# Half-row score products in two banks, and the planner's order for the whole program

## The chip, the cores and the metric

The kernel runs on one core of a Trainium2 chip. The metric is the device time of one execution in microseconds. The kernel before takes 1044.72 us, the median of 3 runs (1044.53 to 1045.08).

## The reference

Attention over a window of 128 positions with a bias by distance, then a feed-forward block (FFN) over the result, all in fp32:

```python
B, H, S, D = 8, 8, 576, 64            # q, k, v: batch, heads, positions, head size
scores = q @ k.T / sqrt(D)            # for each batch and head
scores = where((rel >= 0) & (rel < 128), scores + slope[h] * -abs(rel), -1e9)
attn = softmax(scores)                # over the keys
x = (attn @ v) laid out as [B * S, H * D]       # 4608 x 512
h = x @ w_in                          # 512 x 2048
out = (h * sigmoid(1.702 * h)) @ w_out          # 2048 x 512
```

## The kernel before

**Precision by parts.** TensorE multiplies in fp32r, which is faster than fp32 and rounds its operands. The kernel therefore splits an operand into a rounded high part and the low rest, and adds up several products. In the FFN those are three products per tile (w high with x high, w low with x high, w high with x low; L1074 for the first layer, L1197 for the second, and L1162 in the last chunks, which combine weights first).

**The score products.** A head has 64 dimensions, the array 128 rows. The q and k of a head pair lie in memory twice, once in partitions 0 to 63 and once in 64 to 127. A block is 128 queries with the 256 keys that its window can reach (128 keys for the first block of a sequence). A unit is one or two blocks that are worked on together; a head pair of a batch has 9 blocks, hence 5 units, the last of one block. For each unit the kernel makes the tile Q (rounded q in all partitions, then the low rest of q written over the lower half of the partitions, 64 to 127, L508), K1 (rounded k in both halves) and K2 (the low rest of k in both halves). Each block is then two products on the full array: Q with K1 gives q high times k high plus q low times k high, and Q with K2 adds q high times k low and q low times k low (L853). The two blocks of a unit lie side by side in one bank of PSUM, the tile s_ps, of which there is one.

**After the scores.** VectorE (DVE) adds the bias and finds the row minimum of the negated scores while it reads s_ps (L872), ScalarE (ACT) takes the exponent (L884), the rows are normalised (L907), TensorE transposes them (flip, L928, into one of two t slots of PSUM), ACT and DVE split the transposed tile into high and low (ph, pl, L505 and L947), and TensorE multiplies with V (mix, L973, into x_ps). The sums of head pairs go to the x tiles of the FFN, for later chunks by way of DRAM.

**The first batch** is worked on in plain fp32 (L850 for scores, L967 for the product with V). There the two heads of a pair lie in the two halves of the partitions, so that a score product uses 64 rows of the array, and some of the two heads' products go into two banks, s_ps and s_h.

**The FFN** runs in chunks of 256 tokens over 16 slices of the hidden size: up (12 matmuls into h_ps), the gate (tanh on ACT, L1090; a product on DVE, L1091), the split into gh and gl (L505, L508), down (6 matmuls of 512 columns into two acc banks). The weights come in 8-byte words and are decoded early in the program (w_ps, wc).

**What sets the order.** All work is first added to a list (`Plan.add`) with a duration, the engine, other engines that could do it (`ways`) and what it reads and writes. `Plan.order(CUT)` then plays the list through in its own count of nanoseconds, picks engine, slot and start for each item, and stops at CUT; on PE it takes the item for which `max(free[e], op.ready + SAFE)` is least. What it placed is emitted in that order and stays so. `Plan.rest()` gives out what is left in the order of the list, on the engine named by `auto`, and the framework's scheduler puts these instructions in order by its own simulated timeline. In the kernel before CUT is 340000.

Of the kernel before, what the change touches and what calls it, by code (L numbers as in the profile page):

```python
# [8 lines left out]
F32 = mybir.dt.float32  # L9
# [10 lines left out]
B, H, S, D = 8, 8, 576, 64  # L20
DM, DFF = 512, 2048
NT = B * S
P = 128
HALF = P // 2
NP = H // 2
# [20 lines left out]
GATE = 6  # L46
READY = {"PE": 1600, "DVE": 4400, "ACT": 700, "POOL": 2700, "SP": 700}
HOP = {"PE": 220, "ACT": 60, "DVE": 60, "POOL": 60, "SP": 60}
CUT = 340000
WARM = 7000  # L50
LAX = {"w": 1000, "hi": 800, "lo": 0, "gl": 300, "cast": 0, "xl": 600, "p": 500}
RATE = 330
# [3 lines left out]
MIXED = ("t", "o", "h", "acc1")  # L56
TURN = {}
STICK = 80
SAFE = 60
REST = 400  # L60
FAR = 7
PACE = 32
LATE = 14
FAST = {c: range(0, 7) if c > LATE else range(2, 7) for c in range(LATE, NCH)}
# [202 lines left out]
class Plan:  # L267
# [5 lines left out]
    def add(self, eng, run, ns, lag=100, r=(), w=(), port=False, chain=None, bytes=0, shift=0, ways=None, behind=None, lax=0, auto=None, kind="R", late=None):  # L273
        op = Op(len(self.ops) + shift, eng, run, ns, lag, port)
        op.bytes, op.i = bytes, len(self.ops)
        op.ways.update(ways or {})
        op.lax = lax
        op.auto, op.late = auto or eng, late
        op.kind = kind
        before, after = set(), set()  # L280
        for items, writes in ((r, False), (w, True)):
            for item in items:
                buf, key = item if isinstance(item, tuple) else (item, None)
                if not buf.ops:
                    op.opens.append(buf)
                    if buf.tag not in MIXED:
                        if buf.tag in self.openers:
                            after.add(self.openers[buf.tag])
                        self.openers[buf.tag] = op
                else:  # L290
                    after.add(buf.ops[0])
                buf.ops.append(op)
                buf.left += 1
                op.bufs.append(buf)
                for k in list(buf.last):
                    if meet(key, k):
                        before.add(buf.last[k])
                if writes:
                    for k in list(buf.readers):
                        if meet(key, k):  # L300
                            before.update(buf.readers[k])
                            if key is None or k == key:
                                del buf.readers[k]
                    if key is None:
                        buf.last = {}
                    buf.last[key] = op
                else:
                    buf.readers.setdefault(key, []).append(op)
        if chain is not None:
            if chain in self.chains:  # L310
                after.add(self.chains[chain])
            self.chains[chain] = op
        if behind is not None:
            after.add(behind)
        before.discard(op)
        after -= before | {op}
        for b in sorted(before, key=lambda o: o.i):
            b.next.append((op, True))
        for b in sorted(after, key=lambda o: o.i):
            b.next.append((op, False))  # L320
        op.waits = op.before = len(before) + len(after)
        self.ops.append(op)
        return op
# [141 lines left out]
def tile_kernel(ctx: ExitStack, tc: tile.TileContext, q0, k0, v0, qT, kT, v, w_in, w_out, out):  # L465
    nc = tc.nc
# [9 lines left out]
    add = plan.add  # L476

    def buf(pool, shape, dtype, tag, slots=1, name=None):
        return Buf(plan, pool, shape, dtype, tag, slots, name)
# [9 lines left out]
    def act_cast(n):  # L489
        return 104 + 0.8 * n  # L490
# [10 lines left out]
    def pool_two(n):  # L501
        return 140 + 2.17 * n

    def copy_on(e, dst, src):
        (nc.scalar.copy if e == "ACT" else nc.vector.tensor_copy)(dst, src)  # L505

    def less_on(e, dst, a, b):
        (nc.gpsimd if e == "POOL" else nc.vector).tensor_tensor(dst, a, b, ALU.subtract)  # L508
# [13 lines left out]
    def less_ways(n):  # L522
        return {"DVE": (dve_one(n), True)}
# [246 lines left out]
    def split_q(u):  # L770
        if u.whole:
            return
        u.Q = buf(att, [P, 2 * P], F32R, "Q", 2)
        add("ACT", lambda e: copy_on(e, u.Q.t[:, :u.nq], u.rq.t[:, :u.nq]), act_cast(u.nq), r=[u.rq], w=[u.Q],
            chain="split_q", ways=cast_ways(u.nq), behind=gates[32 * 2 - 1 - 32])

    def split_v(u):
# [10 lines left out]
        for i, c in enumerate(u.loaded):  # L788
            c.vbuf = u.VV
            c.v = lambda i=i, c=c: u.VV.t[:c.n, i].rearrange("p a d -> p (a d)")  # L790

    def split_rest(u):
        if u.whole:
            return
        u.K1 = buf(att, [P, 3 * P], F32R, "K1", 2)
        u.K2 = buf(att, [P, 3 * P], F32R, "K2", 2)
        add("ACT", lambda e: copy_on(e, u.K1.t[:, :u.nk], u.rk.t[:, :u.nk]), act_cast(u.nk),
            r=[u.rk], w=[u.K1], chain="K1", ways=cast_ways(u.nk), auto="DVE")
        add("POOL", lambda e: less_on(
            e, u.Q.t[D:, :u.nq], u.rq.t[D:, :u.nq], u.Q.t[D:, :u.nq].bitcast(F32)), pool_two(u.nq),  # L800
            r=[u.rq], w=[u.Q], port=True, chain="Q", ways=less_ways(u.nq), lax=LAX["lo"])
        add("POOL", lambda e: less_on(
            e, u.K2.t[:, :u.nk], u.rk.t[:, :u.nk], u.K1.t[:, :u.nk].bitcast(F32)), pool_two(u.nk),
            r=[u.rk, u.K1], w=[u.K2], port=True, chain="K2", ways=less_ways(u.nk), lax=LAX["lo"])
# [13 lines left out]

    def scores(u):
        if early(u):  # L820
            u.s = buf(ps, [P, 2, 2 * P], F32, "h", 2, name="s_h")
        else:
            u.s = buf(ps, [P, 2, 2 * P], F32, "s", 1, name="s_ps")
        ns = 0
        runs, reads = [], []
        for e, b in enumerate(u.blocks):
            n = b.end - b.first
            if u.whole:
                lo = b.q0 - u.at
                qr, q = columns(0, u, lo, b.rows)  # L830
                at, k = b.first, lo - P + b.first
                while at < b.end:
                    m = min(b.end - at, T - k % T)
                    kr, ks = columns(1, u, k, m)
                    runs.append((e, b, at, m, q, ks))
                    reads += [r for r in (qr, kr) if r not in reads]
                    ns += max(1.72 * m, 220)
                    at, k = at + m, k + m
            else:
                ko = b.q0 - P + b.first - u.k0  # L840
                qs = slice(b.q0 - u.q0, b.q0 - u.q0 + b.rows)
                ks = slice(ko, ko + n)
                ns += 2 * max(0.465 * n, 86)
                runs.append((e, b, b.first, n, qs, ks))

        def run():
            for e, b, at, n, q, k in runs:
                to = u.s.t[:b.rows, e, at:at + n]
                if u.whole:
                    nc.tensor.matmul(to, q(), k(), start=True, stop=True)  # L850
                else:
                    for z, ks in enumerate((u.K1, u.K2)):
                        nc.tensor.matmul(to, u.Q.t[:, q], ks.t[:, k], start=(z == 0), stop=(z == 1))  # L853

        u.scored = add("PE", run, ns, 165, r=reads if u.whole else [u.Q, u.K1, u.K2], w=[u.s],
            chain="scores", kind="S" if u.whole else "R")
        if early(u):
            u.scored.beside = units[u.n - 1].scored

    def biased(u):  # L860
        u.mins = small(u, 0, "mins")
        for e, b in enumerate(u.blocks):
            if first(u):
                b.p = Part(works[u.n // 2], (u.n % 2, e), lambda t, i=u.n % 2 * 2 + e: t[:, i])
            else:
                b.p = buf(att, [P, 2 * P], F32, "pb", 5)
            for head, ra, rb, cs in b.heads:
                if cs > b.live:
                    add("POOL", lambda b=b, ra=ra, rb=rb, cs=cs: nc.gpsimd.memset(b.p.t[ra:rb, b.live:cs], MOST),
                        230, w=[b.p.key_at()])  # L870
                on = ra if u.joined else 0
                add("DVE", lambda b=b, e=e, head=head, ra=ra, rb=rb, cs=cs, on=on: nc.vector.tensor_tensor_reduce(  # L872
                    b.p.t[ra:rb, cs:b.end], u.s.t[ra:rb, e, cs:b.end], bias[ra:rb, head, on + cs:on + b.end],
                    -SCALE, BIG, ALU.add, ALU.min, u.mins.t[ra:rb, e:e + 1]),
                    75 + 1.05 * (b.end - cs), 150, r=[u.s], w=[b.p.key_at(), u.mins.key_at(e)], chain="biased")
            if b.live > b.first:
                add("POOL", lambda b=b: nc.gpsimd.memset(b.p.t[:, :b.live], 0.0), 120, w=[b.p.key_at("z")])

# [576 lines left out]
```

## Time and profile before

| what | value |
|---|---|
| median of 3 runs | 1044.72 us |
| the profiled execution | 1044.83 us |
| its span, first to last instruction | 1043.0 us |
| busy: PE, DVE, ACT, POOL | 99%, 76%, 63%, 51% |
| granted TensorE clock | 0.999 |
| DMA, mean share of the 16 engines by queue | 31.2% and 2.5%, instructions 0.6% |

A row of a group reads: line, engine, operation, output and inputs, form (rows and columns of the array that a matmul uses, as in 64*128, then the size), count, busy time of the group in microseconds, mean of one in nanoseconds, idle time of the engine ahead of them. The mean of a matmul is its whole way through the array (a matmul of 256 columns shows some 0.28 us); how fast matmuls follow one another is read from their starts. A row of the timeline gives the start, the time to the end of the last one, and the count.

### The profile page before, as it was taken

What the parts mean: (1) busy time and instruction counts of PE and PEld (TensorE: products, weight loads), DVE (VectorE), ACT (ScalarE), POOL (GpSimd) and SP (SyncE); (2) the same over time, 40 slices, a digit from 0 to 9 for tenths busy, and PEclk for the clock granted to TensorE, in tenths of its full rate; (3) what the DMA queues carried; (4) which work ended last, traced back from release to release, by engine and by line L of the source; (5) the groups of instructions that cost most, each with busy time, mean ns of one, the idle gap of its engine ahead of it and who ended that gap; (6) DMA issues with size and microseconds to landing.
All of it is one profiled execution on the core that took longest, in us unless ns stands there. A gap on an engine that the chain in (4) does not pass through costs nothing.

```text
span 1043.0 us, 23177 instructions
## 1 busy us (share of the span) xinstructions
PE 1029.4 (99%) x7220; PEld 937.7 (90%) x7220; DVE 793.5 (76%) x2464; ACT 655.8 (63%) x1962; POOL 530.6 (51%) x804
## 2 busy tenths in 40 slices
PE   9999999999999999999999999999999999999998
PEld 5777888988888999999999999999999999999997
DVE  8999988899978888768686777768766744667574
ACT  7999877677745666666666666666666643344443
POOL 3343445344423467576666757666666623333342
PEclk9999999999999999999999999999999999999999
DMA  9734233333322333434333433424242354001000
GB/s 355 303 96 141 61 88 95 80 81 98 83 76 65 103 101 94 141 90 129 95 114 106 122 104 101 126 76 150 79 117 67 113 169 140 21 22 41 2 22 21
DMA packets 122027, 106.65 MB, mean 102 GB/s; under 512 B 48880, under 2 KB 111984, under 8 KB 121904
## 3 DMA queue, kind: packets, MB, share of 16 engines
q1 hardware_dynamic: 116720, 95.73, 31.2%
q10 hardware_dynamic: 5184, 9.44, 2.5%
q8 instruction: 57, 0.93, 0.4%
q14 instruction: 66, 0.54, 0.2%
HBM read 82.58 MB, written 22.54 MB: 101 GB/s over the span
## 4 chain that ended last, share of the span: by engine, by line
PE 88%; DVE 8%; issue 2%; ACT 2%; POOL 0%; DMA 0%; DVEq 0%; ACTq 0%; POOLq 0%
PE h_ps L1074 35%; PE acc L1197 28%; PE s_ps L853 5%; PE t_ps L928 5%; PE x_ps L973 5%; PE m L1162 3%; PE acc L1162 2%; PE s_ps L850 1%; PE x_ps L967 1%; DVE g L1091 1%; DVE wc L592 1%; DVE pb L872 1%; DVE w_ps L589 1%; PE idle L556 1%; DVE gl L508 1%
## 5 line engine op out<-in xcount | busy, mean ns | idle before, releaser
L1074 PE MATMUL h_ps<-xh,w 128*128 128x256 f32 x2304 | 358.7, 283 | 0.3
L1074 PEld LDWEIGHTS h_ps<-xh,w 128*128 128x128 f32 x2304 | 316.9, 188 | 18.4 <-DVE g L1091 1.7
L1197 PE MATMUL acc<-w,gh 128*128 128x512 f32 x928 | 259.5, 396 | 0.0
L1074 PE MATMUL h_ps<-xl,w 128*128 128x256 f32 x1152 | 187.3, 280 | 0.0
L508 POOL TENSOR_TENSOR gl<-g,gh 128x256 fp32r<-128x256 f32 x169 | 131.7, 781 | 107.5 <-ACT gh L505 68.2
L1197 PEld LDWEIGHTS acc<-w,gh 128*128 128x128 f32 x928 | 157.6, 189 | 19.3 <-issue 0.2
L1074 PEld LDWEIGHTS h_ps<-xl,w 128*128 128x128 f32 x1152 | 158.2, 188 | 2.3
L884 ACT ACTIVATE pb<-pb,mins 128x256 f32<-128x256 f32 (+2 forms) x272 | 132.3, 487 | 39.5 <-DVE mins L872 29.8
L508 POOL TENSOR_TENSOR Q<-rq,Q 64x256 fp32r<-64x256 f32 (+1 forms) x136 | 94.9, 698 | 117.9 <-issue 25.6
L1091 DVE SCALAR_TENSOR_TENSOR g<-g,h_ps 128x256 f32<-128x256 f32 x236 | 97.6, 413 | 72.5 <-ACT g L1090 70.9
L1090 ACT ACTIVATE g<-h_ps 128x256 f32<-128x256 f32 x236 | 90.1, 382 | 92.7 <-PE h_ps L1074 69.7
L1197 PE MATMUL acc<-w,gl 128*128 128x512 f32 x464 | 148.1, 397 | 0.0
L508 POOL TENSOR_TENSOR K<-rk,K 128x384 fp32r<-128x384 f32 (+1 forms) x121 | 109.7, 907 | 69.8 <-ACT Q L505 23.8
L505 ACT CAST gh<-g 128x256 fp32r<-128x256 f32 x184 | 74.6, 405 | 66.8 <-DVE g L1091 60.5
L872 DVE CUSTOM_DVE_ANT_0 pb<-s_ps,bias 128x256 f32<-128x256 f32 (+2 forms) x304 | 110.6, 377 | 5.5 <-PE s_ps L853 1.6
L853 PE MATMUL s_ps<-K,Q 128*128 128x256 f32 (+1 forms) x504 | 92.0, 298 | 2.4 <-DVE mins L872 1.4
L928 PE MATMUL t_ps<-ident,pb 128*128 128x128 f32 x516 | 91.0, 273 | 2.7 <-DVE wc L592 2.4
L505 ACT CAST ph<-t_ps 128x512 fp32r<-128x512 f32 (+2 forms) x133 | 68.8, 518 | 34.3 <-PE t_ps L928 25.7
L1197 PEld LDWEIGHTS acc<-w,gl 128*128 128x128 f32 x464 | 79.3, 188 | 11.8 <-POOL gl L508 0.5
L947 DVE TENSOR_TENSOR pl<-t_ps,ph 128x512 fp32r<-128x512 f32 (+2 forms) x140 | 84.6, 604 | 5.8 <-ACT ph L505 5.3
L907 DVE TENSOR_SCALAR pb<-pb,rec 128x256 f32<-128x256 f32 (+2 forms) x192 | 76.5, 430 | 2.5
L853 PEld LDWEIGHTS s_ps<-K,Q 128*128 128x128 f32 x504 | 69.7, 189 | 8.9 <-DVE mins L872 1.8
(184 smaller groups left out, 1748.3 us busy)
## 6 DMA issues: line engine op xcount, KB each, us to landing
rk<-kT SPq DMA_DIRECT2D x84, 192.0 KB, 2.5
rq<-qT SPq DMA_DIRECT2D x112, 128.0 KB, 2.3
out<-o ACTq DMA_DIRECT2D x34, 256.0 KB, 2.9
rw<-w_in SPq DMA_DIRECT2D x16, 512.0 KB, 8.6
rw<-w_out SPq DMA_DIRECT2D x16, 512.0 KB, 9.5
rk<-kT SPq DMA_DIRECT2D x56, 128.0 KB, 2.2
far<-wmh SPq DMA_DIRECT2D x56, 128.0 KB, 1.9
rv<-v SPq DMA_DIRECT2D x100, 64.0 KB, 2.0
```

The costliest lines, as they stand in the source:

```text
L505: (nc.scalar.copy if e == "ACT" else nc.vector.tensor_copy)(dst, src)
L508: (nc.gpsimd if e == "POOL" else nc.vector).tensor_tensor(dst, a, b, ALU.subtract)
L853: nc.tensor.matmul(to, u.Q.t[:, q], ks.t[:, k], start=(z == 0), stop=(z == 1))
L872: add("DVE", lambda b=b, e=e, head=head, ra=ra, rb=rb, cs=cs, on=on: nc.vector.tensor_tensor_reduce(b.p.t[ra:rb, cs:b.end], u.s.t[ra:rb, e ...
L884: nc.scalar.activation(live, live, AF.Exp, bias=u.mins.t[:b.rows, e:e + 1], scale=-1.0, accum_out=u.sums.t[:b.rows, e, 0:1])
L907: (nc.gpsimd if on == "POOL" else nc.vector).tensor_scalar(live, live, rec, None, ALU.mult)
L928: nc.tensor.transpose(u.t.t[:c.n, w:w + b.rows], b.p.t[:b.rows, col:col + c.n], ident[:b.rows, :b.rows])
L947: add("DVE", lambda m=m, a=a, z=z: nc.vector.tensor_tensor(u.pl.t[:m, a:z], u.t.t[:m, a:z], u.ph.t[:m, a:z].bitcast(F32), ALU.subtract), d ...
L1074: nc.tensor.matmul(h.t, w.t[:, z, k * P:(k + 1) * P], x[k].t, start=(part == 0 and k == 0), stop=(part == 2 and k == NC - 1))
L1090: add("ACT", lambda: nc.scalar.activation(g.t, h.t, AF.Tanh, scale=0.851), act_psum(T), r=[h], w=[g], shift=-NEXT)
L1091: add("DVE", lambda: nc.vector.scalar_tensor_tensor(g.t, g.t, 1.0, h.t, ALU.add, ALU.mult), dve_one(T), r=[h], w=[g], shift=-NEXT)
L1197: nc.tensor.matmul(acc.t, g.t[:, t * P:(t + 1) * P], w.t[:, z], start=new[t], stop=(f == self.f1 - 1 and n == 2), skip_group_check=bool(se ...
```

## The change

Three numbers: CUT becomes 2000000, so that the planner orders the whole program and nothing is left to `rest`; SAFE goes from 60 to 100; ROWS = 2 names the batch from which the new score products are used (`apart`).

For units of batch 2 and later, the low rest of q is written per block: for block 0 into partitions 64 to 127, for block 1 into partitions 0 to 63, so that block 0 has its high q in the upper half and block 1 in the lower one. The product with K1 stays as it was. The product with K2 uses only the 64 rows where the high q lies: block 0 rows 0 to 63, block 1 rows 64 to 127; q low times k low is left out. All K1 products of a unit come first, then the half-row ones. Block 0 has its scores in s_ps, block 1 in a tile s_t in one of the two t slots.

```diff
-CUT = 340000
+CUT = 2000000
-SAFE = 60
+SAFE = 100
+ROWS = 2
...
+    def apart(u):
+        return u.pair // NP >= ROWS
...
-        add("POOL", lambda e: less_on(
-            e, u.Q.t[D:, :u.nq], u.rq.t[D:, :u.nq], u.Q.t[D:, :u.nq].bitcast(F32)), pool_two(u.nq),
-            r=[u.rq], w=[u.Q], port=True, chain="Q", ways=less_ways(u.nq), lax=LAX["lo"])
+        for i, b in enumerate(u.blocks if apart(u) else u.blocks[:1]):
+            at, cols = slice(D, P) if i == 0 else slice(0, D), slice(b.q0 - u.q0, b.q0 - u.q0 + b.rows) if apart(u) else slice(0, u.nq)
+            n = cols.stop - cols.start
+            add("POOL", lambda e, at=at, cols=cols: less_on(
+                e, u.Q.t[at, cols], u.rq.t[at, cols], u.Q.t[at, cols].bitcast(F32)), pool_two(n),
+                r=[u.rq, (u.Q, "all")], w=[(u.Q, i)], port=True, chain="Q", ways=less_ways(n), lax=LAX["lo"])
...
+            u.s = [Part(buf(ps, [P, 2 * P], F32, tag, n, name=name), None, lambda t: t)
+                for b, (tag, n, name) in zip(u.blocks, (("s", 1, "s_ps"), ("t", 2, "s_t")))]
...
-                ns += 2 * max(0.465 * n, 86)
+                ns += max(0.465 * n, 106) if apart(u) else 2 * max(0.465 * n, 86)
...
+        ns += 119 if apart(u) else 0
...
-                else:
+                elif not apart(u):
                     for z, ks in enumerate((u.K1, u.K2)):
                         nc.tensor.matmul(to, u.Q.t[:, q], ks.t[:, k], start=(z == 0), stop=(z == 1))
+                else:
+                    nc.tensor.matmul(to, u.Q.t[:, q], u.K1.t[:, k], start=True, stop=False)
+            if apart(u):
+                for e, b, at, n, q, k in runs:
+                    on = slice(e * D, e * D + D)
+                    nc.tensor.matmul(u.s[e].t[:b.rows, at:at + n], u.Q.t[on, q], u.K2.t[on, k], start=False, stop=True)
```

On TensorE, a unit of the steady part whose first block is a sequence's first. In the kernel before (the planner no longer orders this stretch):

```order
L928 MATMUL t_ps_0_7920<-ident_75,pb_3_7853 128x128
L853 MATMUL s_ps_0_7947<-K1_0_7855,Q_0_7838 128x128
L853 MATMUL s_ps_0_7947<-K2_0_7858,Q_0_7838 128x128
L853 MATMUL s_ps_0_7947<-K1_0_7855,Q_0_7838 128x256
L853 MATMUL s_ps_0_7947<-K2_0_7858,Q_0_7838 128x256
L973 MATMUL x_ps_0_7952<-ph_0_7867,VV_2_7724 128x256
L973 MATMUL x_ps_0_7952<-pl_0_7869,VV_2_7724 128x256
L1197 MATMUL acc0_0_6937<-w2_15_0_2042,gl_1_7783 128x512
```

and in the changed kernel, where L869 is the product with K1, L873 the half-row product with K2, L993 the product with V and L1094 the first FFN layer:

```order
L869 MATMUL s_ps_0_8032<-K1_0_7862,Q_0_7855 128x128
L869 MATMUL s_t_0_8034<-K1_0_7862,Q_0_7855 128x256
L873 MATMUL s_ps_0_8032<-K2_1_7906,Q_0_7855 128x128
L873 MATMUL s_t_0_8034<-K2_1_7906,Q_0_7855 128x256
L993 MATMUL x_ps_0_8042<-ph_0_7956,VV_2_7746 128x256
L993 MATMUL x_ps_0_8042<-pl_1_7976,VV_2_7746 128x256
L993 MATMUL x_ps_0_8042<-ph_0_7956,VV_0_7764 128x256
L993 MATMUL x_ps_0_8042<-pl_1_7976,VV_0_7764 128x256
L1094 MATMUL h_ps_0_8053<-xh0_0_7884,w1_2_0_566 128x256
```

The order within the unit is now K1, K1, K2, K2, and the block with 256 columns is in s_t. Behind the half-row products of a unit stands a product with V in 114 of 120 units, and a first-layer product in 6; always one on the full array.

On VectorE at about the same place. Before:

```order
L1091 SCALAR_TENSOR_TENSOR g_1_7820<-g_1_7820,h_ps_0_7807 128x256
L505 CAST K1_0_8031<-rk_0_7763 128x384
L1091 SCALAR_TENSOR_TENSOR g_0_7903<-g_0_7903,h_ps_1_7890 128x256
L872 ISA pb_2_8026,mins_2_8027<-s_ps_0_7947,bias_76 128x128
L872 ISA mins_2_8027 128x1
L872 ISA pb_0_8029,mins_2_8027<-s_ps_0_7947,bias_76 128x256
L872 ISA mins_2_8027 128x1
L947 TENSOR_TENSOR pl_1_7945<-t_ps_0_7920,ph_1_7943 128x512
```

and in the changed kernel (L1111 is the gate's product, L506 and L509 the casts and low rests, L892 the biased read of the scores):

```order
L1111 SCALAR_TENSOR_TENSOR g_0_8014<-g_0_8014,h_ps_0_7965 128x256
L916 RECIPROCAL rec_1_8018<-rec_1_8018 128x1
L506 CAST gh_1_8027<-g_0_8014 128x256
L637 TENSOR_TENSOR wsum_0_8038<-w2_4_0_747 128x512
L509 TENSOR_TENSOR gl_0_8049<-g_0_8014,gh_1_8027 128x256
L967 TENSOR_TENSOR pl_0_8058<-t_ps_1_8022,ph_1_8040 128x512
L509 TENSOR_TENSOR VV_2_8060<-rv_1_7799,VV_2_8060 128x64
L892 ISA pb_0_8074,mins_1_8075<-s_ps_0_8032,bias_76 128x128
L892 ISA mins_1_8075 128x1
L892 ISA pb_2_8080,mins_1_8075<-s_t_0_8034,bias_76 128x256
L892 ISA mins_1_8075 128x1
```

The split of the gate's result (gh, gl) and low rests of V and K now stand in VectorE's list, where the kernel before had them on ACT and POOL in this stretch. Over the program VectorE's list grows from 2450 to 2817 rows, and POOL's shrinks from 806 to 575, ACT's from 1686 to 1586.

More of the change, by code (lines that the diff above doesn't have):

```diff
@@ L773, in split_q @@
         u.Q = buf(att, [P, 2 * P], F32R, "Q", 2)
-        add("ACT", lambda e: copy_on(e, u.Q.t[:, :u.nq], u.rq.t[:, :u.nq]), act_cast(u.nq), r=[u.rq], w=[u.Q],
+        add("ACT", lambda e: copy_on(e, u.Q.t[:, :u.nq], u.rq.t[:, :u.nq]), act_cast(u.nq), r=[u.rq], w=[(u.Q, "all")],
             chain="split_q", ways=cast_ways(u.nq), behind=gates[32 * 2 - 1 - 32])
@@ L820, in scores @@
         if early(u):
-            u.s = buf(ps, [P, 2, 2 * P], F32, "h", 2, name="s_h")
-        else:
-            u.s = buf(ps, [P, 2, 2 * P], F32, "s", 1, name="s_ps")
+            s = buf(ps, [P, 2, 2 * P], F32, "h", 2, name="s_h")
+        elif not apart(u):
+            s = buf(ps, [P, 2, 2 * P], F32, "s", 1, name="s_ps")
+        if not apart(u):
+            u.s = [Part(s, None, lambda t, e=e: t[:, e]) for e in range(len(u.blocks))]
+        else:
+            u.s = [Part(buf(ps, [P, 2 * P], F32, tag, n, name=name), None, lambda t: t)
+                for b, (tag, n, name) in zip(u.blocks, (("s", 1, "s_ps"), ("t", 2, "s_t")))]
         ns = 0
@@ L842, in scores @@
                 ks = slice(ko, ko + n)
-                ns += 2 * max(0.465 * n, 86)
+                ns += max(0.465 * n, 106) if apart(u) else 2 * max(0.465 * n, 86)
                 runs.append((e, b, b.first, n, qs, ks))
+        ns += 119 if apart(u) else 0
         def run():
             for e, b, at, n, q, k in runs:
-                to = u.s.t[:b.rows, e, at:at + n]
+                to = u.s[e].t[:b.rows, at:at + n]
                 if u.whole:
                     nc.tensor.matmul(to, q(), k(), start=True, stop=True)
-                else:
+                elif not apart(u):
                     for z, ks in enumerate((u.K1, u.K2)):
                         nc.tensor.matmul(to, u.Q.t[:, q], ks.t[:, k], start=(z == 0), stop=(z == 1))
-        u.scored = add("PE", run, ns, 165, r=reads if u.whole else [u.Q, u.K1, u.K2], w=[u.s],
+                else:
[4 more added lines that the diff above has]
+                    nc.tensor.matmul(u.s[e].t[:b.rows, at:at + n], u.Q.t[on, q], u.K2.t[on, k], start=False, stop=True)
+        u.scored = add("PE", run, ns, 165, r=reads if u.whole else [u.Q, u.K1, u.K2], w=[x.buf for x in u.s[:2 if apart(u) else 1]],
             chain="scores", kind="S" if u.whole else "R")
@@ L872, in biased @@
                 add("DVE", lambda b=b, e=e, head=head, ra=ra, rb=rb, cs=cs, on=on: nc.vector.tensor_tensor_reduce(
-                    b.p.t[ra:rb, cs:b.end], u.s.t[ra:rb, e, cs:b.end], bias[ra:rb, head, on + cs:on + b.end],
+                    b.p.t[ra:rb, cs:b.end], u.s[e].t[ra:rb, cs:b.end], bias[ra:rb, head, on + cs:on + b.end],
                     -SCALE, BIG, ALU.add, ALU.min, u.mins.t[ra:rb, e:e + 1]),
-                    75 + 1.05 * (b.end - cs), 150, r=[u.s], w=[b.p.key_at(), u.mins.key_at(e)], chain="biased")
+                    75 + 1.05 * (b.end - cs), 150, r=[u.s[e].buf], w=[b.p.key_at(), u.mins.key_at(e)], chain="biased")
             if b.live > b.first:
```

## The prediction

> **What bounds the kernel now.** I read first the page's busy times, then the engines by stretches of time: one that the planner's order covers already (200 to 300 us) and one behind it (457 to 514 us, one FFN chunk of the steady part).
>
> ```profile
> PE 1029.4 (99%) x7220; PEld 937.7 (90%) x7220; DVE 793.5 (76%) x2464; ACT 655.8 (63%) x1962; POOL 530.6 (51%) x804
> ...
> 200.00:300.00 100.00, 98.12 (x677) 88.17 (x676) 89.78 (x333) 69.43 (x209) 41.72 (x71) 1.00 0.31 84
> 457.00:514.00 57.00, 57.00 (x396) 52.77 (x395) 43.65 (x131) 36.27 (x117) 37.16 (x57) 1.00 0.38 110
> ```
>
> Columns of the lower rows: stretch, length, then busy time of PE, PEld, DVE, ACT and POOL. PE is busy all through, but its ends are modelled, so I ask instead how many matmuls a stretch holds and at what pace they can follow each other. The chain of waits gives the pace of unbroken runs, and the timeline that of transposes:
>
> ```profile
> 423.08 2.77 PE acc L1197 x12
> ...
> 482.94 1.42 PE h_ps L1074 x12
> ...
> 503.37 0.60 PE L928 MATMUL t_ps<-ident,pb 128*128 128x128 f32 x4
> ```
>
> 2.77/12 = 0.231 us per matmul of 512 columns and 1.42/12 = 0.118 per one of 256. Four transposes show 0.60; with the last one's 0.272 (row below) off, three steps take 0.328, so 0.109 each. Now the counts, by groups of PE, of 457 to 514 us and below them of 200 to 300 us:
>
> ```profile
> L1074 PE MATMUL h_ps<-xh,w 128*128 128x256 f32 x128 | 21.0, 284 | 0.0
> L1197 PE MATMUL acc<-w,gh 128*128 128x512 f32 x64 | 18.0, 396 | 0.0
> L1074 PE MATMUL h_ps<-xl,w 128*128 128x256 f32 x66 | 10.9, 279 | 0.0
> L1197 PE MATMUL acc<-w,gl 128*128 128x512 f32 x32 | 10.3, 397 | 0.0
> L853 PE MATMUL s_ps<-K,Q 128*128 128x256 f32 (+1 forms) x36 | 6.4, 296 | 0.0
> L928 PE MATMUL t_ps<-ident,pb 128*128 128x128 f32 x34 | 6.2, 272 | 0.0
> L973 PE MATMUL x_ps<-ph,VV 128*128 128x256 f32 (+1 forms) x18 | 4.7, 278 | 0.0
> L973 PE MATMUL x_ps<-pl,VV 128*128 128x256 f32 (+1 forms) x18 | 4.7, 281 | 0.0
> ...
> L1074 PE MATMUL h_ps<-xh,w 128*128 128x256 f32 x202 | 28.5, 280 | 0.1
> L1197 PE MATMUL acc<-w,gh 128*128 128x512 f32 x100 | 27.3, 394 | 0.0
> L1074 PE MATMUL h_ps<-xl,w 128*128 128x256 f32 x103 | 16.5, 282 | 0.0
> L1197 PE MATMUL acc<-w,gl 128*128 128x512 f32 x50 | 15.6, 394 | 0.0
> L853 PE MATMUL s_ps<-K,Q 128*128 128x256 f32 (+1 forms) x76 | 14.1, 303 | 0.9 <-DVE mins L872 0.6
> L928 PE MATMUL t_ps<-ident,pb 128*128 128x128 f32 x70 | 11.4, 272 | 0.0
> L973 PE MATMUL x_ps<-ph,VV 128*128 128x256 f32 (+1 forms) x38 | 10.2, 287 | 0.9 <-ACT K L505 0.4 <-DVE xf L1037 0.4
> L973 PE MATMUL x_ps<-pl,VV 128*128 128x256 f32 (+1 forms) x38 | 9.6, 280 | 0.0
> ```
>
> Steady part: 194 h at 0.118, 96 acc at 0.231, 72 scores and products with V at about 0.117, 34 transposes at 0.109: 22.9 + 22.2 + 8.4 + 3.7 = 57.2 us of 57.0. TensorE streams without a hole; whatever the change adds to its stream there is added to the time, and a better order has nothing to win. In the planned stretch 305, 150, 152 and 70 of them make 36.0 + 34.7 + 17.8 + 7.6 = 96.1 of 100 us: 3.9 us per 100 are lost, with DVE at 90% and the waits on DVE and ACT in the last column.
>
> **The score products.** From the third batch on (ROWS = 2) a unit multiplies Q with K1 on the full array and with K2 on one half of the rows per block, the two halves in two banks. That is 6 batches of 4 head pairs with 5 units each: 72 with two full blocks, 24 whose first block has 128 columns, 24 with one block, 120 in all. The first batch of the kernel before already multiplies halves side by side (s_ps and s_h, L850), so the trace shows both what the pairing gives and what it asks for:
>
> ```profile
> 11.12 0.37 PE L850 MATMUL s_h<-k,q 64*128 64x128 f32 x1
> 11.14 0.37 PE L850 MATMUL s_ps<-k,q 64*128 64x128 f32 x1
> 11.34 0.27 PE L850 MATMUL s_h<-k,q 64*128 64x128 f32 x1
> ...
> 11.45 0.38 PE L850 MATMUL s_h<-k,q 64*128 64x256 f32 x1
> ...
> 11.67 0.38 PE L850 MATMUL s_h<-k,q 64*128 64x256 f32 x1
> ...
> 11.99 0.33 PE L928 MATMUL t_ps<-ident,work 128*128 128x128 f32 x1
> ...
> 41.87 1.20 PE L1074 MATMUL h_ps<-xh,w 128*128 128x256 f32 x8
> 42.91 0.62 PE L1074 MATMUL h_ps<-xl,w 128*128 128x256 f32 x4
> 43.45 1.14 PE L850 MATMUL s_ps<-k,q 64*128 64x128 f32 x6
> 44.53 0.66 PE L928 MATMUL t_ps<-ident,pb 128*128 128x128 f32 x4
> ```
>
> The pairing is real: the partner starts 0.01 to 0.02 us later (11.12, 11.14) and the pairs follow at 0.11 (128 columns, 11.34 to 11.45) and 0.22 (256 columns, 11.45 to 11.67), plain fp32 at about twice the 0.118 of fp32r. But a change between 128*128 and 64*128 has a price on each side. Ahead of it: the four at 42.91 pace at (0.62 - 0.279)/3 = 0.114, yet 43.45 starts 0.54 after the first, so the last took 0.20, 0.09 more. Inside: six half-row products from 43.45 to 44.53 take 1.08; by their paces 4 x 0.11 + 2 x 0.22 = 0.88, so 0.20 more (at 11.12 it shows split: the first pair 0.22 for 0.11, the last 0.32 for 0.22). Behind: the eight at 41.87, after products of form 128*64, take 1.04 for 8 x 0.118 = 0.94, 0.10 more. One visit to the half-row form thus costs 0.09 + 0.20 + 0.10 = 0.39 us, on the engine that has no hole to hide it in. In the changed order each of the 120 units makes such a visit by itself: K1 products ahead, and x_ps or h_ps on the full array behind.
>
> Sum, at 0.118 per 256 columns and 0.11 per 128. Two full blocks: 4 x 0.118 = 0.472 before; 2 x 0.118 + 0.118 + 0.013 + 0.39 = 0.757 after: +0.285, x72 = 20.5. First block short: 0.456 before, 0.11 + 0.118 + 0.131 + 0.39 = 0.749 after: +0.293, x24 = 7.0. One block: 0.236 before, 0.118 + 0.118 + 0.39 = 0.626 after: +0.39, x24 = 9.4. Together +36.9 us.
>
> Not shown is a half-row product in fp32r. From below: only the two prices that fall on fp32r products in these rows count (0.09 ahead, 0.10 behind), 0.19 a visit, 120 x 0.20 = 24 us less: +13. From above: all of 0.39. I take the upper one, since the rows show the same 0.1 on fp32 and on fp32r neighbours; below both lies "no price at all", a rival.
>
> The Trainium skill ("TensorEngine Tiling (Array Packing)", Key Properties) says that changing the tiling mode, not just the tile, drains TensorE, and gives no price; "TensorE: Matmul & The Clock Gate", Single matmul latency, has 398 cycles at 2.4 GHz beyond the columns, 0.166 us. With that as the price of each of 240 changes the term would be 39.8 instead of 46.8 us and the time, by this estimate, 1083. The row has a duration, so the row decides.
>
> **POOL and the banks.** The low half of Q is now cut into two instructions of 64x128 for each two-block unit:
>
> ```profile
> L508 POOL TENSOR_TENSOR Q<-rq,Q 64x256 fp32r<-64x256 f32 x108 | 79.8, 739 | 88.5 <-issue 24.2 <-ACT K L505 17.5 <-ACT ph L505 7.6
> L508 POOL TENSOR_TENSOR Q<-rq,Q 64x128 fp32r<-64x128 f32 x28 | 15.2, 541 | 29.4 <-DVE wsum L636 18.8 <-ACT K L505 5.5 <-DVE mins L872 1.6
> ```
>
> 2 x 0.541 - 0.739 = 0.34 us, x96 = 33 us of POOL, which is 51% busy and whose list gets shorter (575 rows for 806): nothing, or 33 us if that cover were gone. The second score bank is one of the two t slots; flips wait until DVE has read it. That is late next if DVE is late, and is part of the next term.
>
> **The planned order for all.** CUT now lies behind the end, so the stretch after the first third loses the order that the framework made and gets the planner's; it shifts work from POOL and ACT to DVE (2817 rows for 2450; gl and gh among them). It can't win: 57.2 of 57.0. It can lose what 200 to 300 us loses: 3.9 per 100 over the 700 us from 343 on, 27 us. SAFE = 100 acts in the same choice. DVE decides where between: 90% there, 77% (43.65 of 57) in the steady part. The 367 added rows at the page's mean of 793.5/2464 = 0.322 us are +118 us of DVE, (793 + 118)/1090 = 84% over all, about halfway; I go nearer to the easy end, because every visit also makes TensorE 0.3 us later than the planner counts. I take 0.3 of the way: +8 us.
>
> **Sum.** The profiled execution took 1044.83 us (span 1043.0), 0.1 above the median of the runs: 1044.8 + 36.9 + 8 = 1090 us.
>
> **Rivals.**
> Half-row products in fp32r change the form for nothing. For it: one tile form changes free of charge already, transposes of 64 rows out:
>
> ```profile
> L928 PE MATMUL t_ps<-ident,pb 128*64 128x128 f32 x4 | 1.1, 272 | 0.0
> ...
> 66.27 0.41 PE L928 MATMUL t_ps<-ident,pb 128*128 128x128 f32 x2 [0.60 <-DVE wc L592]
> 66.44 0.72 PE L1074 MATMUL h_ps<-xl,w 128*128 128x256 f32 x4
> ```
>
> The second of the two at 66.27 is of that form, and h_ps follows 0.17 later. Against it: those are transposes; the real products at 11.12 and 43.45 pay on both sides, and so do fp32r neighbours. Then 96 pairs save 0.118 - 0.013 each, -10 us: 1035 with no loss from the order, 1043 with 8. From a visit price below some 0.02 us (2 us gained over 8) this ends faster. Chance 0.14. The skill's tiling page promises up to twice the speed for 64 rows, and its TensorE page 4 ns per further tile; the 13 ns here alter the sum by 0.9 us.
>
> Half price: only the fp32r neighbours pay, 1044.8 + 13 + 8 = 1066. Chance 0.13.
>
> The planner's order stalls as in 200 to 300 us: 1044.8 + 36.9 + 27 = 1109. For it: DVE gets the work. Against it: the delays above give DVE time. Chance 0.12.
>
> The change doesn't do what it says, the halves run one after the other: +0.118 x 96 = 11 us, 1101. The partner 0.02 us behind at 11.14 speaks against it. Chance 0.04.
>
> **The numbers.** The forecast, 1075 to 1100, has the remaining 0.57. The range of 1056 to 1111 takes in half price and the stalling order and leaves out mainly the free change. A measurement here tells 0.2% (2 us) from no change: faster by more 0.10, within it 0.04, slower by more 0.86; only the free change feeds the first two.
>
> **What would show it.** Right: rows of form 64*128 on the K2 line in pairs 0.01 to 0.02 us apart, the last K1 product taking about 0.21 instead of 0.118, x_ps starting about 0.3 after the pair, and the same matmuls of the steady part spread over some 6% more time. Wrong: x_ps 0.13 behind the pair and K1 at 0.118 (free change), or PE waits on DVE mins and xs of several us per 100 (planner). DVE above 90% would say that I put the planner's term too low.

## The result and the profile after

The changed kernel takes 1092.65 us (median of 4 runs, 1092.59 to 1092.74) against 1044.81 for the kernel before on the same chip: the ratio is 1.0459, with a 95% interval of 1.0444 to 1.0475. It is slower by 47.8 us; the forecast was 1090 us with a range of 1056 to 1111.

The busy times on the page of the changed kernel, and in the second fence two stretches of its steady part (length, then PE, PEld, DVE, ACT, POOL):

```profile
PE 1077.4 (99%) x7220; PEld 946.1 (87%) x7220; DVE 848.9 (78%) x2831; ACT 660.0 (61%) x1861; POOL 364.1 (33%) x634
```

```profile
400.00:500.00 100.00, 99.56 (x652) 87.12 (x651) 84.68 (x287) 62.17 (x177) 30.94 (x59) 1.00 0.35 100
500.00:600.00 100.00, 99.12 (x644) 86.00 (x643) 82.49 (x282) 59.47 (x168) 27.94 (x55) 1.00 0.35 102
```

PE looks as busy as before, and it has the same 7220 matmuls. What changed is how many of them fit into 100 us: 652 and 644, where the kernel before had 396 in 57 us, so 695. The timeline of PE at one two-block unit of the steady part shows why (L869 is the product with K1, L873 the half-row product with K2, L993 the one with V):

```profile
501.98 0.36 PE L869 MATMUL s_ps<-K,Q 128*128 128x256 f32 x1
502.18 0.28 PE L869 MATMUL s_t<-K,Q 128*128 128x256 f32 x1
502.38 0.38 PE L873 MATMUL s_ps<-K,Q 64*128 64x256 f32 x1
502.39 0.38 PE L873 MATMUL s_t<-K,Q 64*128 64x256 f32 x1
502.70 0.39 PE L993 MATMUL x_ps<-ph,VV 128*128 128x256 f32 x1
502.92 0.28 PE L993 MATMUL x_ps<-pl,VV 128*128 128x256 f32 x1
503.04 0.76 PE L1094 MATMUL h_ps<-xh,w 128*128 128x256 f32 x5
```

The two half-row products start 0.01 us apart, so they do run side by side. But the last K1 product (502.18) holds the array for 0.20 instead of 0.118, the pair for 0.32, and the first product with V behind it for 0.22: 0.08 + 0.20 + 0.10 = 0.38 us for the visit to the other form, to save one product of 0.118. (The first K1 product, behind the transposes, shows 0.20 as well, but it does so with full rows too, in the next fence, so that is no part of the visit.)

### The profile page after: what moved, and what is told of

Read it like the earlier page. It is cut to its first block, busy times and chain, and to the rows that moved or that the text cites. A ratio compares the mean times of both kernels' runs of the same rounds, so it can differ in the third digit from the quotient of the medians.

```text
span 1090.8 us, 23454 instructions
## 1 busy us (share of the span) xinstructions
PE 1077.4 (99%) x7220; PEld 946.1 (87%) x7220; DVE 848.9 (78%) x2831; ACT 660.0 (61%) x1861; POOL 364.1 (33%) x634
## 4 chain that ended last, share of the span: by engine, by line
PE 88%; DVE 8%; issue 2%; ACT 1%; POOL 1%; DVEq 0%; POOLq 0%; ACTq 0%
PE h_ps L1094 34%; PE acc L1217 26%; PE x_ps L993 7%; PE t_ps L948 5%; PE m L1182 3%; PE s_ps L873 3%; PE acc L1182 3%; DVE pb L892 1%; PE s_ps L864 1%; PE s_t L869 1%; PE s_ps L869 1%; PE x_ps L987 1%; DVE pl L967 1%; DVE g L1111 1%; PE s_ps L867 1%
## 5 line engine op out<-in xcount | busy, mean ns | idle before, releaser
L1094 PE MATMUL h_ps<-xh,w 128*128 128x256 f32 x2304 | 331.3, 284 | 0.1
L1094 PEld LDWEIGHTS h_ps<-xh,w 128*128 128x128 f32 x2304 | 300.7, 188 | 12.2 <-DVE g L1111 2.8
L509 POOL TENSOR_TENSOR Q<-rq,Q 64x128 fp32r<-64x128 f32 (+1 forms) x220 | 106.6, 484 | 400.8 <-issue 117.8
L1094 PE MATMUL h_ps<-xl,w 128*128 128x256 f32 x1152 | 185.7, 283 | 0.0
L1094 PEld LDWEIGHTS h_ps<-xl,w 128*128 128x128 f32 x1152 | 157.9, 188 | 1.7 <-issue 0.2
L1111 DVE SCALAR_TENSOR_TENSOR g<-g,h_ps 128x256 f32<-128x256 f32 x236 | 98.1, 416 | 56.1 <-ACT g L1110 53.8
L925 ACT ACTIVATE pb<-pb,rec 128x256 f32<-128x256 f32 (+2 forms) x152 | 73.0, 485 | 68.7 <-DVE rec L916 67.4
L506 ACT CAST ph<-t_ps 128x512 fp32r<-128x512 f32 (+2 forms) x111 | 59.7, 538 | 82.6 <-PE t_ps L948 80.4
L509 DVE TENSOR_TENSOR gl<-g,gh 128x256 fp32r<-128x256 f32 x214 | 95.5, 446 | 8.8 <-ACT gh L506 1.6
L993 PE MATMUL x_ps<-ph,VV 128*128 128x256 f32 (+1 forms) x264 | 81.1, 325 | 4.7 <-DVE rec L913 2.4
L509 POOL TENSOR_TENSOR K<-rk,K 128x384 fp32r<-128x384 f32 (+1 forms) x75 | 71.7, 956 | 34.3 <-ACT pb L904 11.4
L892 DVE CUSTOM_DVE_ANT_0 pb<-s_ps,bias 128x256 f32<-128x256 f32 (+5 forms) x208 | 76.2, 368 | 6.7 <-PE s_t L873 3.0
L948 PEld LDWEIGHTS t_ps<-ident,pb 128*128 128x128 f32 x516 | 64.1, 140 | 19.0 <-issue 1.4
L993 PEld LDWEIGHTS x_ps<-ph,VV 128*128 128x128 f32 x264 | 49.5, 187 | 27.3 <-issue 5.8
```

What stands on the lines that cost most here:

```text
L925: nc.scalar.activation(live, live, AF.Copy, scale=rec)
L948: nc.tensor.transpose(u.t.t[:c.n, w:w + b.rows], b.p.t[:b.rows, col:col + c.n], ident[:b.rows, :b.rows])
L993: nc.tensor.matmul(g.x.t[:, a:a + c.width], c.v(), p.t[:m, s:e], start=(c is g.first and z == 0), stop=(c is g.last and z == 1), skip_grou ...
L1094: nc.tensor.matmul(h.t, w.t[:, z, k * P:(k + 1) * P], x[k].t, start=(part == 0 and k == 0), stop=(part == 2 and k == NC - 1))
L1111: add("DVE", lambda: nc.vector.scalar_tensor_tensor(g.t, g.t, 1.0, h.t, ALU.add, ALU.mult), dve_one(T), r=[h], w=[g], shift=-NEXT)
```

## The experiments

My theory was the prediction's: each visit to the half-row form costs 0.39 us on an engine without a hole, and the planner's order costs some more. The rivals: the banks, POOL's longer chain or the planner's order make the loss, or each half-row product pays and not the visit.

### Full rows in the changed order

```diff
-                    on = slice(e * D, e * D + D)
+                    on = slice(0, P)
```

K2 is the same in both halves of the partitions, so the product over all rows is that of the kernel before, and no instruction changes its place.

> The changed kernel with one thing undone: the product with K2 runs on all 128 rows again (K2 is the same in both halves, so the sum is that of the kernel before). The order of every engine, the two banks, the cut low rests of Q and the waits stay as in the changed kernel. My theory (a visit to the half-row form costs 0.39 us on TensorE, which has no hole): 120 x 0.39 = 46.8 us go, and 96 pairs lose their overlap, 96 x 0.105 = 10.1 us come: 1092.7 - 46.8 + 10.1 = 1056 us. Rival (the banks, POOL's longer chain or the planner's order make the loss): 1085 us or more.

Measured: 1066.65 us (ratio 1.0211, 1.0195 to 1.0226). The row form alone is worth 26.0 us in this order, so the rival that it is worth nothing falls; but I had expected 36.7, and 1066.65 lies 10.6 above what my sum gave. The timeline of this kernel at a two-block unit:

```profile
502.11 0.36 PE L869 MATMUL s_ps<-K,Q 128*128 128x256 f32 x1
502.31 0.28 PE L869 MATMUL s_t<-K,Q 128*128 128x256 f32 x1
502.43 0.29 PE L873 MATMUL s_ps<-K,Q 128*128 128x256 f32 x1
502.55 0.28 PE L873 MATMUL s_t<-K,Q 128*128 128x256 f32 x1
502.66 0.28 PE L993 MATMUL x_ps<-ph,VV 128*128 128x256 f32 x1
502.78 0.28 PE L993 MATMUL x_ps<-pl,VV 128*128 128x256 f32 x1
```

From the last K1 product to the second one with V it takes 0.47 us here and 0.74 (502.18 to 502.92) in the changed kernel. At the unit the full 0.27 is there; some of it comes back elsewhere. Both kernels have the same matmuls in the same order, so their starts can be compared one by one. From the last K1 product to the second matmul behind the half rows, the 120 visits make the changed kernel 34.8 us longer in all (the median is 0.277 us for a two-block unit and 0.387 for a single block). Outside the visits it is 8.8 us shorter, 5.1 of them just ahead of products with V and 2.6 just ahead of products of the second FFN layer; 26.0 is left. PE's waits between 200 and 900 us (what waited for whom: total, times, longest) show some of where. The first three rows, with full rows and then in the changed kernel:

```profile
PE x_ps L993 <- DVE rec L913: 4.4, 10, 0.7
PE x_ps L993 <- POOL K L509: 2.2, 5, 0.5
PE x_ps L993 <- DVE xs L1034: 0.7, 2, 0.4
```

```profile
PE x_ps L993 <- DVE rec L913: 2.4, 10, 0.5
PE x_ps L993 <- POOL K L509: 1.2, 5, 0.3
PE x_ps L993 <- ACT K L506: 0.4, 1, 0.4
```

The same ten and five waits are there in both, and about half as long where TensorE comes to them later. All rows of this view together make 9.8 us with full rows and 4.2 in the changed kernel.

### The planner's order alone

```diff
-ROWS = 2
+ROWS = 99
```

> CUT = 2000000 and SAFE = 100 alone; the score products as in the kernel before (ROWS = 99). My theory: the planner's order loses some 8 us behind the first third, 1053 us, and at most 27 us (1071). Rival (the planner's order as good as the framework's, and all of the loss comes from the half rows): 1045 to 1047 us.

Measured: 1066.49 us (1.0207, 1.0190 to 1.0224). The order for the whole program costs 21.7 us by itself: inside the bound of 27, far from my 8, and the rival that it costs nothing falls. Full rows has the two banks and the cut low rests, which this kernel has not, and an order that the planner made anew for them; all of that together is worth 0.2 us, less than the runs of either kernel differ among themselves. Taken in this sequence, the loss divides into 21.7 for the order, 0.2 for banks and POOL, and 26.0 for the row form.

### The half rows alone

```diff
-CUT = 2000000
+CUT = 340000
-SAFE = 100
+SAFE = 60
```

> The half-row products alone, with CUT = 340000 and SAFE = 60 as before. In the part that the framework orders, it puts other matmuls between the two half-row products of 36 of the 96 two-block units, so that there are 156 visits and 60 pairs. My theory: 1044.8 + 36.9 + 36 x (0.39 + 0.105) = 1099.5 us, more than the whole change. Rival (the planner's order carries a large part of the loss): below 1085 us.

Measured: 1097.23 us (1.0507, 1.0490 to 1.0524), 2 below what was expected and slower than the whole change. The timeline shows one unit that the framework took apart, and the row below it a stretch of the steady part:

```profile
410.22 0.36 PE L869 MATMUL s_ps<-K,Q 128*128 128x256 f32 x1
410.52 0.38 PE L873 MATMUL s_ps<-K,Q 64*128 64x256 f32 x1
410.83 0.39 PE L993 MATMUL x_ps<-pl,VV 128*128 128x256 f32 x1
411.05 0.28 PE L1094 MATMUL h_ps<-xh,w 128*128 128x256 f32 x1
411.17 0.28 PE L869 MATMUL s_t<-K,Q 128*128 128x256 f32 x1
411.38 0.38 PE L873 MATMUL s_t<-K,Q 64*128 64x256 f32 x1
411.69 0.62 PE L1094 MATMUL h_ps<-xh,w 128*128 128x256 f32 x3
```

```profile
400.00:500.00 100.00, 100.00 (x632) 85.80 (x632) 73.85 (x215) 59.24 (x189) 63.17 (x106) 1.00 0.34 97
```

In this unit each half-row product makes its own visit (0.31 from 410.52 and from 411.38) and nothing overlaps; only 632 matmuls fit into 100 us. Over the program the trace has the 156 visits and 60 pairs that were expected. Here the stream has almost no holes (PE's listed waits between 200 and 900 us add up to 0.9 us), and the visits cost about what the rows said. So the planner's order does one thing for the half rows: it keeps a unit's products together. Taken in this sequence the half rows cost 52.4 us and the planner's order takes 4.6 off again: neither has a price by itself that holds whatever the other does.

### The pair twice in one visit

```diff
-                for e, b, at, n, q, k in runs:
+                for z, (e, b, at, n, q, k) in [(z, x) for z in range(2) for x in runs]:
...
-                    nc.tensor.matmul(u.s[e].t[:b.rows, at:at + n], u.Q.t[on, q], u.K2.t[on, k], start=False, stop=True)
+                    nc.tensor.matmul(u.s[e].t[:b.rows, at:at + n], u.Q.t[on, q], u.K2.t[on, k], start=False, stop=z == 1)
```

> The changed kernel with the half-row products of each unit issued twice in the same visit (q high times k low is then added twice). My theory (the price is paid per visit, not per product): 96 x 0.13 + 24 x 0.118 = 15 us more, 1108 us. Rival (each half-row product or pair pays its 0.2 to 0.39 us): 1092.7 + 120 x 0.39 or more, 1140 us; with 0.2 per pair 1092.7 + 15 + 24 = 1132.

Measured: 1107.39 us (1.0598, 1.0582 to 1.0614), 14.7 more than the changed kernel, as the price per visit has it; a price per pair falls. The timeline of one visit:

```profile
508.91 0.28 PE L869 MATMUL s_t<-K,Q 128*128 128x256 f32 x1
509.12 0.38 PE L873 MATMUL s_ps<-K,Q 64*128 64x256 f32 x1
509.12 0.38 PE L873 MATMUL s_t<-K,Q 64*128 64x256 f32 x1
509.34 0.28 PE L873 MATMUL s_ps<-K,Q 64*128 64x256 f32 x1
509.34 0.28 PE L873 MATMUL s_t<-K,Q 64*128 64x256 f32 x1
509.55 0.39 PE L993 MATMUL x_ps<-ph,VV 128*128 128x256 f32 x1
```

One pair held the array 0.32 (502.38 to 502.70 above), two hold it 0.43: the second adds 0.11.

### What makes the planner's order slow

Two edits of the planner's order alone. The first keeps the low rest gl on POOL:

```diff
-            add("POOL", lambda e: less_on(e, gl.t, g.t, gh.t.bitcast(F32)),
-                697, r=[g, gh], w=[gl], port=True, shift=-NEXT, ways=less_ways(T), lax=LAX["gl"],
+            add("POOL", lambda: less_on("POOL", gl.t, g.t, gh.t.bitcast(F32)),
+                697, r=[g, gh], w=[gl], port=True, shift=-NEXT, lax=LAX["gl"],
```

> The planner's order alone as in e2 (1066.5 us), with the low rest gl of the FFN's gate kept on POOL as the framework's part of the kernel before has it; some 174 instructions of 0.445 us leave DVE. Theory (the planner's order stalls TensorE because it loads DVE to 89% in the steady part): the 3 to 4 us lost per 100 fall to 1 or 2, 1052 to 1058 us. Rival (not the load but the fixed order, with waits that the framework would have worked around): 1064 us or more, since a gl on POOL takes 0.34 us longer.

Measured: 1059.28 us (1.0141, 1.0119 to 1.0163), above what the theory gave and below the rival. The stretches from 400 to 600 us, first of the planner's order alone, then with gl on POOL:

```profile
400.00:500.00 100.00, 98.81 (x670) 89.06 (x669) 89.62 (x279) 62.08 (x181) 40.83 (x61) 1.00 0.34 98
500.00:600.00 100.00, 99.34 (x674) 89.87 (x673) 88.08 (x276) 63.44 (x182) 39.67 (x59) 1.00 0.39 112
```

```profile
400.00:500.00 100.00, 99.43 (x681) 90.65 (x680) 80.48 (x261) 65.02 (x188) 55.26 (x81) 1.00 0.36 104
500.00:600.00 100.00, 99.09 (x677) 90.07 (x676) 77.78 (x256) 65.89 (x188) 52.19 (x80) 1.00 0.38 109
```

DVE goes from 89 to 79%, and 679 matmuls fit where 672 did and the framework's order has 695. Of the 21.7 us 7.2 went. The stretches with gl on POOL are from an execution of 1063.1 us, above the median, which began slower (106 matmuls in its first 25 us, where the planner's order alone had 132); the stretches shown lie behind that. The load of DVE is a part of the loss, if the moved instructions are the reason and not another order that came with them; what makes the other two thirds stays open, and that it is the fixed order as such was not shown.

The second edit takes SAFE back:

```diff
-SAFE = 100
+SAFE = 60
```

> The planner's order alone, SAFE = 60 as before instead of 100. Theory (the loss is the planner's order for the steady part): within 3 us of 1066.5. Rival (the larger margin delays the choice on TensorE and makes the loss): 1050 us or less.

Measured: 1070.45 us (1.0250, 1.0226 to 1.0273), some 4 us slower than with 100 and so just outside the 3 us of the theory. The larger margin doesn't make the loss; it takes a little off it.

### Less of the planner's order

If the framework loses less than the planner, the planner could stop earlier in the kernel before.

```diff
-CUT = 340000
+CUT = 200000
```

> The kernel before with CUT = 200000: the framework orders the stretch from 200 us on as well. Theory (the planner loses 3.9 us per 100 from 200 to 300 us and some 1 in the 40 behind, the framework almost nothing): 1040 to 1042 us, faster than both kernels. Rival (that stretch is bound by something else, such as the batches' due times, and the loss only moves): 1044 us or more.

Measured: 1046.56 us (1.0011, 1.0001 to 1.0022): no gain; my theory was wrong here and the rival's time came. And the value between the two, CUT = 270000:

> The kernel before with CUT = 270000, between the two. Theory: half of the gain of CUT = 200000, 1042.5 us. Rival: 1044 us or more.

Measured: 1042.76 us (0.9976, 0.9967 to 0.9985), faster than the kernel before by a little (0.24%). The same stretches show how the two differ; first CUT = 200000 (200 to 300, 300 to 340, 340 to 400 us), then 270000 (200 to 300, 300 to 340), last the kernel before (340 to 400):

```profile
200.00:300.00 100.00, 97.30 (x679) 88.76 (x678) 83.55 (x279) 66.79 (x220) 68.26 (x108) 1.00 0.30 83
300.00:340.00 40.00, 38.87 (x268) 35.30 (x267) 27.40 (x91) 26.17 (x84) 24.66 (x39) 1.00 0.30 83
340.00:400.00 60.00, 58.90 (x408) 53.99 (x407) 44.19 (x147) 37.97 (x125) 39.98 (x61) 1.00 0.36 101
```

```profile
200.00:300.00 100.00, 98.53 (x686) 89.22 (x685) 88.81 (x328) 70.43 (x216) 47.95 (x79) 1.00 0.31 85
300.00:340.00 40.00, 40.00 (x278) 37.01 (x278) 25.65 (x85) 25.46 (x80) 24.54 (x37) 1.00 0.28 79
```

```profile
340.00:400.00 60.00, 59.60 (x419) 54.88 (x419) 51.17 (x163) 40.22 (x127) 36.56 (x52) 1.00 0.37 103
```

With CUT = 200000 the framework too leaves holes: 679 matmuls from 200 to 300 us where the kernel before has 677, and 408 from 340 to 400 where that has 419. So the framework's order is not without loss everywhere; it was almost without loss in the part that it had.

## Why the prediction was right or wrong

**The floor of TensorE: right.** That 57 us held 57.2 us of matmuls said that a better order had nothing to win and that whatever is added to the stream is added to the time. The half rows alone, +52.4 us for an expected 54.7, bear it out for the framework's order. For the planner's order, which the change brings with it, it doesn't hold, as the fourth point here says.

**The price of a visit: right.** 0.39 us was read off plain fp32 products of the first batch (its last part, 0.10, behind products of form 128*64, not 64*128); the fp32r visit shows 0.38, and the timeline has the three parts in the places that were named. The rivals "free change" and "half price" fall with that row, and "one after the other" with 502.38 and 502.39. Full rows in the same order, 26.0 us faster, makes it a cause and not a coincidence. By its size alone 26.0 would lie between half price (13) and the full 36.9; the rows of the timeline and the 34.8 us at the visits decide. Measured are 0.08 us on the product ahead, 0.20 on the pair itself and 0.10 on the product behind. With that the trace agrees with the rule of the Trainium skill ("TensorEngine Tiling (Array Packing)", Key Properties) that a change of the tiling mode drains TensorE.

**POOL and the banks: right, at nothing.** 0.2 us between full rows and the planner's order alone. One 64x128 rest took 0.464 us, not 0.541. POOL's list got shorter, though by less than was said: the two pages count 804 instructions before and 634 after, not 575.

```profile
L509 POOL TENSOR_TENSOR Q<-rq,Q 64x128 fp32r<-64x128 f32 x204 | 94.7, 464 | 382.7 <-issue 111.3 <-DVE Q L506 57.1 <-ACT Q L506 50.7
```

**The planner's term: mis-sized, and the sum of the two terms not a sum.** "+8 us" was the choice between 0 and 27. By itself the order costs 21.7. The visits' 36.9 as reckoned and these 21.7 make 58.6; together the two cost 47.8. The step that failed is that a visit falls "on the engine that has no hole to hide it in": that is so in the framework's order, but the planner's order leaves TensorE waiting for data, and a TensorE that comes later waits less. So the row form costs 26.0 us there and not 36.9; 8.8 us of the difference are the time that came back between the visits. The prediction named this effect as its reason to go nearer to the easy end ("every visit also makes TensorE 0.3 us later than the planner counts"), and in that reading its 8 stands against 47.8 - 36.9 = 10.9. But it worked out no size for the effect. That the total came within 3 us is in part luck: the order by itself costs 13.7 more than forecast, the row form in that order 10.9 less. For the planner's order alone the same numbers would have said 1053, and it takes 1066.

**DVE's load.** 84% of the span was forecast and 78% came (848.9 us of 1090.8). The 367 more instructions came, but with 55 us and not 118, since work also left DVE: against 147 more gl of 0.446 us and 111 more gh of 0.345, 77 normalised blocks of about 0.42 us and 54 casts of K of 0.42 us went, nearly all to ACT, and 88 of the added instructions are short sums of 0.15 us. In the stretches from 400 to 800 us DVE is at 82 to 85%, and at 86 to 90% in the planner's order alone. The sign that the prediction named for a planner's term put too low, DVE above 90%, didn't show in them, and for the order by itself the term was too low all the same.

## What to carry to other kernels

Before half-row products are set side by side, count the visits: a visit costs 0.39 us here, and a pair of 256 columns saves some 0.11, so by estimate about four pairs have to share one visit before anything is gained; two is the most that was run. Read a candidate's cost from a place where the same kernel already does the thing; ten rows from the first 45 us held the price of a visit. And costs on one engine add up only while its stream has no holes: measure two edits apart and together before giving each its share.

## What the runs showed of the hardware

The price of a visit to the half-row form came out the same for fp32 and fp32r products (0.39 and 0.38 us a visit, with the part behind the fp32 products taken from another form), and it is paid once per visit: the first pair in a visit takes 0.32 to the next full-row product, a second pair 0.11 more. A pair takes no longer than one half-row product by itself (0.32 from 502.38, 0.31 from 410.52). The partner in the other half of the rows starts 0.00 to 0.01 us behind in the timeline. I had expected the price, but not that a stream with waits of its own would swallow so much of it: of 34.8 us at the visits 8.8, or a quarter, came back where TensorE would otherwise have waited, in the listed rows mostly for DVE and POOL.
